# An interleaved attention and MLP kernel: another fixed table of order, engine choices and buffer places

## The chip, the cores and the metric

The kernel runs on one core of a Trainium2 chip. The metric is the device time of one execution in microseconds (us). The time before is the median of 3 runs, 1171.26 us (1171.18 to 1172.04). A core has a matrix engine (TensorE, PE in the profile; its weight loads are PEld), three engines for other arithmetic (VectorE or DVE, ScalarE or ACT, GpSimd or POOL), and a queue that issues transfers (SyncE or SP, SPq in the profile).

## What is computed

Two kinds of layer alternate on x, 2048 rows by 512 features in fp32. `_layernorm` subtracts the mean of a row and divides by its standard deviation.

```python
def _A_ref(x, wqkv, wo):                     # H = 32 heads of Dh = 16
    W, dil = 8, 2
    q, k, v = (x @ wqkv).reshape(B, S, 3, H, Dh).transpose(2, 0, 3, 1, 4)
    idx = pos[:, None] - (arange(W) * dil)[None, :]    # 8 earlier rows, every 2nd
    logits = einsum("bhsd,bhswd->bhsw", q, k[idx]) * Dh ** -0.5
    attn = softmax(where(idx >= 0, logits, -1e9))
    return einsum("bhsw,bhswd->bhsd", attn, v[idx]) @ wo     # heads joined

def _B_ref(x, w1, w2, w3, w4):               # F = 1792
    h = gelu(layernorm(x) @ w1)
    # four quarters of the features, moved by +1, -1, +2, -2 rows
    x1 = x + shifted(h) @ w2
    return x1 + gelu(layernorm(x1) @ w3) @ w4

for layer in range(2):
    x = x + _A_ref(layernorm(x), wqkv, wo)
    x = x + _B_ref(layernorm(x), w1, w2, w3, w4)
```

## The kernel before

**Tiling.** The 2048 rows are cut into 4 blocks of 4 tiles of 128 rows. A step number n counts pairs of layer and block, from 0 to 7; "block 3" or `p4[0]` in this text means the step with that n. An fp32 product is made from fp16 parts: a weight, or a transposed activation, is split in a high and a low half (`w_hl`, `wo_hl`, `wq_hl`; `nT`, `xt`, `oT`), and three products, high by high, high by low, low by high, are added up. A tile by a 512x512 weight is so a group of twelve matmuls of 512 columns.

**Stages.** At the start the weights come in, are scaled by a power of two and are split: for w3 and w4, pair by pair (`big_pair`, line 932), the squares are summed into `ss_p`, a matmul with `ones` adds them over the partitions, DVE reads the sum as `mx`, and a scale `inv_p` follows; `small_weight` (line 910) does the same for wo, w1 and w2. `p1_quarters` (line 793) makes q, k and v of block 0 from fp32 weights at once. `p1_stream` (line 854) does so for each later n: it normalises and transposes x to `xt`, runs the qkv groups `mm<-wq_hl,xt` and writes them to a scratch in DRAM (`kvq_d`). `p2_unit` (line 1004) is the attention of one tile, on DVE mostly: it loads the shifted rows (`kv`), multiplies (`prod<-kv,q`), reduces (`L<-prod`), takes the softmax, multiplies again (`prod<-kv,L`) and adds up. For n of 0 and 1 PE does part of the adding, by `mm<-ident,prod`. The attention of one n is called a set here. `p3` (line 1156) is the product with wo (`mm<-wo_hl,oT`), the layernorm, the product with w1 (`mm<-nT,w_hl`), gelu and the row shifts. `p4` (line 1277) is the product with w2 (`mm<-w_hl,h`), the sum `f<-mm,s_w,f` and the second layernorm. `p5` (line 1342) is the MLP: `mm<-nT,w` makes the hidden features, `acc<-w,g` the output.

**Turning a tile.** Every activation must be transposed before a matmul takes it as weights. `split_turned` and `turn_any` (lines 652 and 670) know three ways. In T_PE, PE transposes the fp32 tile in four pieces (`mm<-ident,f`), ACT copies the high half out, PE subtracts it in the bank (`mm<-nT,minus_id`, called the correction here) and ACT copies out what is left. T_SUB transposes on PE too and subtracts on DVE. T_DMA casts the tile to fp16 (`g<-f`), takes the remainder on POOL or DVE (`g<-f,g`) and has SP issue a transposing transfer (`nT<-g`, `xt<-g`, `oT<-g`).

**What sets the order.** The kernel first describes a graph of 3793 operations, each with one or more ways: the engine that does it, or the kind of PSUM bank it uses (`mm` or `acc`). The function `plan` then runs them by a fixed table. A number k in `ORDER` names operation k // 4 and its way k % 4; each engine gets its instructions in the order of the table and runs them in that order (the class `InOrder`, whose `issue` at line 348 is the line of every instruction in the profile, so groups are told apart by tile names). `SLOTS` holds one hexadecimal digit for each buffer: its place in the pool of its kind. `KEEP` names the operation ahead of which `fill` puts warm-up matmuls, and how many; the first 38 (`WARM`) come ahead of everything.

```python
    for b, c in zip(bufs.values(), "".join(SLOTS.split()), strict=True):
        b.t = slots[b.kind][int(c, 16)]
    for k in ORDER:
        o = ops[k // 4]
        if k // 4 in KEEP:
            todo.append(lambda o=o, n=KEEP[k // 4]: fill(o, n))
        todo.append(o.alts[k % 4][1])
```

A buffer in a place waits until all users of the buffer that was there are done, whichever engines they are on. An engine that waits holds up everything behind it in its own order.

Of the kernel before, what the change touches and what calls it, by code (L numbers as in the profile page):

```python
# [238 lines left out]
4116420101235127621133433326510212035335  # L239
"""  # L240

KEEP = {22: 26}


class Buf:
# [65 lines left out]
def plan(ops, slots, fill=None, picks=()):  # L311
# [11 lines left out]
    for k in ORDER:  # L323
        o = ops[k // 4]
        assert o.before | o.order <= done
        done.add(o)
# [1136 lines left out]
```

## Time and profile before

| | |
|---|---|
| median of 3 runs | 1171.26 us |
| the profiled execution | 1171.19 us |
| its span | 1169.4 us |
| its mean granted PE clock | 0.995 |
| busy PE, DVE, ACT, POOL | 1149.4, 893.0, 597.4, 414.0 us |
| DMA | 206.04 MB, mean 176 GB/s |

A row of a group reads: line, engine, operation, tiles (out<-in) and shape, count, then busy time, mean ns of one, and the idle time before them with what ended it. The mean ns of one matmul is longer than its share of the busy time, because matmuls overlap in the array. A row of a timeline reads: start, length, engine, operation, count, and in brackets the idle time before it and what ended that. In the rows of transfers the last number is the median of us from issue to landing.

### The profile page before, as it was taken

Reading aid. Unit: us, or ns where it says so; the run is one execution under the profiler, and the core shown is the slowest. Engines: PE = TensorE matmul, PEld = TensorE weight load, DVE = VectorE, ACT = ScalarE, POOL = GpSimd, SP = SyncE. Lnnn points to the kernel's source line nnn. Section 1 sums busy time; section 2 is a strip of 40 time slices with the busy share of each in tenths; the row PEclk is TensorE's granted clock in tenths of the full one; section 3 lists DMA queues with packets and bytes.
Section 4 is the critical chain, followed back from the end, with each engine's and each line's share of the span. In section 5 each row is a group of like instructions: output and inputs, shape, how many; then the busy total and the mean of one; then the engine's idle time right before and its main releaser. Section 6 shows DMA issues by size and latency. Waiting matters only on the chain.

```text
span 1169.4 us, 15821 instructions
## 1 busy us (share of the span) xinstructions
PE 1149.4 (98%) x5688; PEld 562.9 (48%) x5688; DVE 893.0 (76%) x1074; ACT 597.4 (51%) x1149; POOL 414.0 (35%) x480
## 2 busy tenths in 40 slices
PE   9999999899999999999999999999999999999998
PEld 7545556455444444444444444444444444444554
DVE  6799988999998995499957989999825999325112
ACT  6665657556664656343553456455544564253232
POOL 3555354424345335332523241731332152223000
PEclk9999999899999999999999999999999999999999
DMA  7678986555586737764568488765378466333312
GB/s 252 214 230 281 271 257 207 187 194 178 161 209 186 168 96 184 226 167 127 162 177 282 136 205 219 189 170 155 102 195 216 129 169 194 103 100 86 98 70 99
DMA packets 231990, 206.04 MB, mean 176 GB/s; under 512 B 104108, under 2 KB 157604, under 8 KB 231912
## 3 DMA queue, kind: packets, MB, share of 16 engines
q1 hardware_dynamic: 231036, 204.07, 61.3%
q8 instruction: 44, 0.72, 0.3%
q10 hardware_dynamic: 876, 0.97, 0.2%
q14 instruction: 34, 0.28, 0.1%
HBM read 141.03 MB, written 39.47 MB: 154 GB/s over the span
## 4 chain that ended last, share of the span: by engine, by line
PE 79%; DVE 8%; DMA 7%; issue 2%; ACT 2%; SPq 1%; POOL 1%; DVEq 0%; ACTq 0%; POOLq 0%
PE mm L348 56%; PE acc L348 23%; DMA kvq_d<-ev 3%; DVE prod L348 3%; DVE L L348 2%; DMA q<-kvq_d 1%; SPq L348 1%; DMA kv<-kvq_d 1%; DVE wq_hl L348 1%; ACT junk L348 1%; DMA w<-w 1%; ACT ev L348 0%; DMA h<-in_B_w_dram 0%; DMA w<-g 0%; DVE mx L348 0%
## 5 line engine op out<-in xcount | busy, mean ns | idle before, releaser
L348 POOL TENSOR_TENSOR g<-f,g 128x512 f16<-128x512 f32 (+1 forms) x123 | 175.0, 1430 | 355.4 <-ACT g L348 158.1
L348 PE MATMUL acc<-w,g 128*128 128x512 f16 x1302 | 298.0, 379 | 0.0
L348 PE MATMUL mm<-nT,w 128*128 128x512 f16 (+1 forms) x1344 | 296.7, 374 | 0.9 <-ACT nT L348 0.7
L348 ACT ACTIVATE mm<-mm,s_w 128x512 f32<-128x512 f32 (+2 forms) x158 | 97.9, 622 | 252.9 <-PE mm L348 252.6
L348 PEld LDWEIGHTS <-w 128*128 128x128 f16 x1512 | 142.0, 98 | 155.3 <-issue 4.5
L348 PEld LDWEIGHTS <-g 128*128 128x128 f16 x1398 | 137.3, 98 | 158.9 <-issue 1.9
L348 PE MATMUL mm<-wq_hl,xt 128*128 128x512 f16 x732 | 164.5, 379 | 1.0 <-DVE ev L348 1.0
L348 PEld LDWEIGHTS <-xt 128*128 128x128 f16 x1008 | 98.5, 98 | 116.9 <-issue 1.5
L348 DVE TENSOR_REDUCE L<-prod 128x128 f32<-128x2048 f32 (+1 forms) x44 | 142.5, 3248 | 0.5
L348 DVE TENSOR_TENSOR prod<-kv,q 128x4096 f32<-128x4096 f32 (+1 forms) x32 | 117.9, 3683 | 6.1 <-DMA kv<-kvq_d 3.6
L348 DVE SCALAR_TENSOR_TENSOR g<-mm,c_g,g 128x512 f16<-128x512 f32 (+1 forms) x53 | 39.3, 743 | 83.1 <-ACT g L348 82.0
L348 DVE TENSOR_TENSOR prod<-prod 128x1024 f32<-128x1024 f32 (+2 forms) x56 | 93.6, 1672 | 0.8
L348 DVE TENSOR_TENSOR prod<-kv,L 128x4096 f32<-128x4096 f32 (+1 forms) x23 | 86.2, 3751 | 1.9 <-PE acc L348 1.6
L348 PE MATMUL mm<-wo_hl,oT 128*128 128x512 f16 x384 | 86.6, 379 | 0.4 <-DVE g L348 0.3
L348 PE MATMUL mm<-nT,w_hl 128*128 128x512 f16 x384 | 86.1, 379 | 0.6 <-DVE g L348 0.6
L348 PE MATMUL mm<-w_hl,h 128*128 128x512 f16 x384 | 85.8, 379 | 0.0
L348 ACT ACTIVATE g<-mm,c_g 128x512 f16<-128x512 f32 (+1 forms) x112 | 74.1, 673 | 2.5
L348 PEld LDWEIGHTS <-oT 128*128 128x128 f16 x426 | 41.4, 98 | 49.1 <-issue 1.2
L348 PE MATMUL acc<-wq_hl,xt 128*128 128x512 f16 x276 | 62.5, 379 | 0.0
L348 PEld LDWEIGHTS <-w_hl 128*128 128x128 f16 x384 | 37.5, 98 | 45.9 <-issue 1.3
L348 PEld LDWEIGHTS <-h 128*128 128x128 f16 x384 | 37.5, 98 | 45.2 <-DVE h L348 0.4
L348 ACT ACT_TABLE_LOAD x40 | 51.3, 1283 | 5.3 <-PE mm L348 3.9
(250 smaller groups left out, 1338.5 us busy)
## 6 DMA issues: line engine op xcount, KB each, us to landing
w<-w SPq DMA_DIRECT2D x224, 256.0 KB, 4.2
kv<-kvq_d SPq DMA_DIRECT2D x62, 768.0 KB, 6.5
kvq_d<-ev SPq DMA_DIRECT2D x84, 256.0 KB, 3.6
w<-in_B_w_dram SPq DMA_DIRECT2D x28, 256.0 KB, 3.8
w<-g SPq DMA_DIRECT2D x28, 256.0 KB, 4.9
q<-kvq_d SPq DMA_DIRECT2D x28, 256.0 KB, 4.1
w<-in_A_x_dram SPq DMA_DIRECT2D x16, 256.0 KB, 4.0
x<-in_A_x_dram SPq DMA_DIRECT2D x16, 256.0 KB, 4.7
```

The lines of the kernel that those rows point to most:

```text
L348: i = f(*a, **k).ins
```

## The change

Three tables change and nothing else. `ORDER` has another sequence, and 550 of the 3793 operations have another way. `SLOTS` has other digits. The warm-up matmuls of `KEEP` move from operation 22 (the transposes of tile 0 of block 0) to operation 33 (those of tile 1).

```diff
 ORDER = [int(k) for k in """
-952 16 40 32 37 24 52 956 20 64 29 45 60 48 69 76 196 72 81 209 152 85 158 202 164 160 204 213 168 108 88 114 116 96
...
 SLOTS = """
...
-KEEP = {22: 26}
+KEEP = {33: 26}
```

Among the other ways: 5 of the tiles that PE transposed are now turned by DMA (3 in `p1_stream`, 2 in `p3`), so there are 20 fewer `mm<-ident,f`, 7 fewer corrections by `minus_id`, and 5 more DMA transposes (`nT<-g` 49 to 51, `xt<-g` 17 to 20). In `p4` some tiles change their way in both directions. Of the 32 adds `x<-x,f` DVE does 19 (8 before) and POOL 13 (24 before).

**VectorE, some 60 us in (place B).** These rows of DVE lead to the read of the power sum `ss_p_225` of the second pair of w3 and w4, which is `mx_264<-mm_70` before and `mx_256<-mm_72` after. L is the logits of the first attention set, junk the dump of a square. Before:

```order
L348 SCALAR_TENSOR_TENSOR junk,ss_p_225<-w_292 128x512
L348 TENSOR_REDUCE L_296<-prod 128x16x8 x2
L348 TENSOR_SCALAR inv_w_237<-inv_w_237 128x1 x2
L348 TENSOR_TENSOR L_296<-L_296,maskb 128x256
L348 TENSOR_SCALAR mx_255<-mm_68 128x1
L348 TENSOR_SCALAR mx_264<-mm_70 128x4
L348 TENSOR_TENSOR prod<-kv_273,x_278 128x2048
```

After:

```order
L348 TENSOR_REDUCE L_296<-prod 128x16x8
L348 TENSOR_SCALAR x_286<-acc_270,s_kv 128x128
L348 TENSOR_SCALAR x_287<-acc_270,s_kv 128x128
L348 TENSOR_TENSOR L_296<-L_296,maskb 128x256
L348 TENSOR_REDUCE mx_255<-L_296 128x32
L348 SCALAR_TENSOR_TENSOR junk,ss_p_225<-w_248 128x512
L348 TENSOR_SCALAR x_286<-mm_70,s_kv 128x128
L348 SCALAR_TENSOR_TENSOR junk,ss_p_225<-w_291 128x512
L348 TENSOR_SCALAR mx_267<-mm_72 128x1
L348 TENSOR_SCALAR inv_w_237<-inv_w_237 128x1 x2
L348 TENSOR_SCALAR mx_256<-mm_72 128x4
```

The two reduces stood between the last square and the read, and now stand ahead of the squares. On PE the power sum is still followed by a group of twelve `mm<-wq_hl,g` and then the four transposes that take the same bank (`mm_70` before, `mm_72` now).

**TensorE, from `p4[0]` to `p5[0]` (place C).** These are the rows of PE from the last w2 matmul of block 0 to its first MLP matmul; the nT of the last row is the second layernorm of three tiles. Before:

```order
L348 MATMUL mm_72<-w_hl,h_254 128x512
L348 MATMUL mm_68<-ident,f_289 128x128 x4
L348 MATMUL mm_66<-ident,f_265 128x128 x4
L348 LDWEIGHTS minus_id
L348 MATMUL mm_68<-nT_287,minus_id 128x512
L348 LDWEIGHTS minus_id
L348 MATMUL mm_66<-nT_287,minus_id 128x512
L348 MATMUL mm_72<-ident,f_265 128x128 x4
L348 LDWEIGHTS minus_id
L348 MATMUL mm_72<-nT_287,minus_id 128x512
L348 LDWEIGHTS w_248
L348 MATMUL mm_72<-nT_287,w_248 128x384
```

After, with the other eleven matmuls of each qkv group left out:

```order
L348 MATMUL mm_72<-w_hl,h_253 128x512
L348 LDWEIGHTS minus_id
L348 MATMUL mm_68<-oT_268,minus_id 128x512
L348 MATMUL mm_70<-ident,f_260 128x128 x4
L348 MATMUL mm_72<-ident,f_264 128x128 x4
L348 LDWEIGHTS minus_id
L348 MATMUL mm_70<-nT_288,minus_id 128x512
...
L348 MATMUL acc_273<-wq_hl,xt_301 128x512
...
L348 MATMUL mm_72<-nT_288,minus_id 128x512
...
L348 MATMUL acc_275<-wq_hl,xt_301 128x512
...
L348 MATMUL mm_72<-nT_288,w_282 128x384
```

Two groups of qkv matmuls of a later block now stand between the corrections and the first MLP matmul, and the third tile's transposes and correction are gone from PE: that tile is turned by DMA. The row with `oT_268` is a correction of another tile that stood elsewhere before.

More of the change, by code (lines that the diff above doesn't have):

```diff
@@ L44 @@
 ORDER = [int(k) for k in """
[174 rows of a table removed]
[174 rows of a table added]
 """.split()]
 SLOTS = """
-714320110422530132632313030201112100021110201233010283600023337540332314113200107520031330113335011321210130511060200
-033425024357010002022155361243020107010413322144030501023153041530040501022033214603060201013641123535000403031451354
-606405061200100320032130101033011002000201021020032110110131100100120000000041202201213205030120111330203002000103111
-202110113311023200103331112000011311002111011011023001100130112120102000112211002030000000000353203302115110220111211
@@ L225 @@
-002410133032051240311003001120101030020114011011101122000053012321112030100620102300100131002100000000213612120002140
-251203111005010131310010502103102120011220011133001111010211001121100601120001100220106301000100221310132624800231510
-316300262010031202230010351030413033473020136050151623604407110453541326207336221235053740211526326130401116351020020
-630533204020021000132300020001012242051022051651040123336361235323425735006011633001705422423532376210011555604242334
-300000124201001103331011010300021304021111020102000103203101530102010133000113211210010120101160010100113313100614267
@@ L230 @@
-305216002231013320404012124301115200311020422530336735031204041120335045471106300210371360650234211022614103630457035
-200000020001021310421110030303010311111001000010010110222100400213001020301010312023011232301111021010102121010423815
-102300204212012220536203122005104000511120232410035401610230150710325204031246043150576165351165103020245041121575231
-300000011000120203611202151331010214021100011002121011303011231103210020200113101001100310201000012111013231101226204
-100102101161000120512200214100200310206530034220430431230126122050517140340605103623117151522630022422476013251540320
@@ L235 @@
-600003100002100102620011041053001301102101030110020102213101110122310130130106211212011113001023000221000313100507381
-202316100130031100100112301203313530136210133430330335120137110422051343670302115310574060212464102151204232540173202
-650623011052002220233005052030110002055302044101223005342045132072303101401222720160310516642523202572132133463653701
-521400374830401330034000000042631021510331213003330023543053013023021112361230070321353012423411603223151622733523211
-4116420101235127621133433326510212035335
+103760101101101233421522032510210011220112322133201131603101254031112251231200200482002031202100121200403352407010204
@@ new lines @@
+000335115643070102031014412234000702010322051606040500022623124545030401011133022016070002011001343551050406021622412
+355631713211001100002110100103321122020201033201102000100101201110030000000051341002200115004301210001502133011020141
+353310211100022111022010120121012110133120010110022211103230102131103300103010023100000000050130011113010132230010130
+303301133000141342203313301122201122221106311131001002200001020031011132001421221211121331112000000000112022111032100
+331310000002031221300011502330111110001000100212001032112330113223101530000310013111006001123101020101131735230531310
@@ new lines @@
+005201143040410302420531300022033022403060317161150443435526134470416032112057511043233030005135467040232354041620500
+230115003152021201321520420630023443022501012570542310634220261130114200576162131322416010112710536342402611621403131
+500003024003011010521013011101120311035302101121321010112011000022301020310101211012011000101063012330102131011313758
+302314101213053020321103020205113210122300014120526724332012135512243043063021233570236064201515041730164261730451201
+000002016102101513411313020351130204001010110101120101212011520202001112001001312122100003201160020110113213100110214
@@ new lines @@
+103006001343030500431311230302200320231530135410332435730215231620253102202434051171246062502160051702251161641321252
+000001131001111312120200110030101105130011100021131013031010001203101001220116112221100321201113010000111300010225763
+202214002001043400502201203000011200412130434510020320132014351760120261530016320700423235070134354512376141143560200
+500004004212010411611013030362011202124213021121200103210010210200010113030110302112010032010062102310112013010308201
+002304303032033310432211035001103020201330135400026701212304101103553010300267265243017040343176032502624304163304220
@@ L240 @@
+367542043132023600414101342011300042161304115102353304216152301210645632732120134231224735560320710123653623750526420
+120225380230000220235003142013121310530311101022443001310020441000033143302310360100421221170310502503371101642213162
+2133000205703134124206216020322116705234
 """
-KEEP = {22: 26}
+KEEP = {33: 26}
 class Buf:
```

347 rows, old and new, of the table ORDER are left out of this document.

## The prediction

> **What bounds the kernel now.** I read the page first (the totals and the chain), then TensorE's waits, then clock and busy time by windows, then the two places that the windows pick out.
>
> ```profile
> span 1169.4 us, 15821 instructions
> PE 1149.4 (98%) x5688; PEld 562.9 (48%) x5688; DVE 893.0 (76%) x1074; ACT 597.4 (51%) x1149; POOL 414.0 (35%) x480
> PE 79%; DVE 8%; DMA 7%; issue 2%; ACT 2%; SPq 1%; POOL 1%; DVEq 0%; ACTq 0%; POOLq 0%
> ```
>
> PE is busy for 98% of the span and holds 79% of the chain. Only two things can shorten this kernel: less matmul work, or less of the 20 us of idle PE (1169.4 − 1149.4) and of the half-clock time that idling brings. The profiled execution took 1171.19 us, so 1.8 us lie around the span; it stands 0.07 below the median of 1171.26, and I make the sum against it.
>
> ```profile
> PE mm L348 <- DVE mx L348: 2.4, 1, 2.4
> PE mm L348 <- POOL f L348: 2.3, 3, 1.1
> PE mm L348 <- ACT nT L348: 1.8, 3, 0.7
> ...
> 60.00:70.00 10.00, 7.62 (x38) 4.02 (x36) 8.67 (x15) 3.47 (x9) 6.31 (x5) 0.83 0.69 204
> ...
> 210.00:220.00 10.00, 6.78 (x34) 3.50 (x31) 9.45 (x10) 7.66 (x19) 6.67 (x11) 0.89 0.82 280
> 220.00:230.00 10.00, 9.31 (x50) 5.67 (x50) 7.94 (x9) 3.88 (x6) 0.56 (x1) 0.76 0.27 65
> ...
> 350.82:409.29 58.47, 58.47 (x275) 26.80 (x273) 54.16 (x45) 30.33 (x52) 26.39 (x20) 1.00 0.67 177
> 935.00:1000.00 65.00, 65.00 (x305) 29.76 (x304) 59.65 (x54) 29.57 (x53) 23.70 (x16) 1.00 0.62 172
> ```
>
> The first three rows are TensorE's longest waits. The others are windows: length, then busy time of PE, weight load, DVE, ACT and POOL, then granted clock. From 60 to 70 us, and from 210 to 230 us, PE idles and the clock is below one; in the other two it never stops. There DVE is busy 54.16 of 58.47 us and 59.65 of 65: a second engine stands just behind PE.
>
> **Place B, 58 to 69 us**: PE, then DVE.
>
> ```profile
> 58.58 2.11 PE L348 MATMUL mm<-wq_hl,g 128*128 128x384 f16 x12
> 63.08 0.63 PE L348 MATMUL mm<-ident,f 128*128 128x128 f32 x4 [2.38 <-DVE mx L348]
> 63.54 3.32 PE L348 MATMUL acc<-wq_hl,g 128*128 128x384 f16 x12
> ...
> 57.12 0.69 DVE L348 SCALAR_TENSOR_TENSOR junk<-w 128x512 bf16<-128x512 f32 x1 [4.76 <-ACT junk L348]
> 57.74 4.47 DVE L348 TENSOR_REDUCE L<-prod 128x128 f32<-128x2048 f32 x2
> 62.71 0.22 DVE L348 TENSOR_SCALAR mx<-mm 128x1 f32<-128x1 f32 x2
> ```
>
> Four transposes need the bank in which a power sum lies until DVE has read it as mx, and DVE first does two reduces of 4.47 us. PE stands for 2.38 us; then twelve matmuls that took 2.11 us take 3.32. The window's clock of 0.83 is a loss of 0.17 × 10 = 1.7 us, so place B costs 2.4 + 1.7 = 4.1 us.
> [...]
>
> **Place C, 213 to 224 us**, the hand-over from the first block's w2 matmuls to its MLP.
>
> ```profile
> 213.77 0.60 PE L348 MATMUL mm<-ident,f 128*128 128x128 f32 x4
> 215.30 0.66 PE L348 MATMUL mm<-ident,f 128*128 128x128 f32 x4 [0.93 <-POOL f L348]
> ...
> 216.64 0.38 PE L348 MATMUL mm<-nT,minus_id 128*128 128x512 f16 x1 [0.47 <-ACT nT L348]
> 218.15 1.12 PE L348 MATMUL mm<-ident,f 128*128 128x128 f32 x4 [1.14 <-POOL f L348]
> 219.95 0.58 PE L348 MATMUL mm<-nT,minus_id 128*128 128x512 f16 x1 [0.69 <-ACT nT L348]
> 221.22 5.60 PE L348 MATMUL mm<-nT,w 128*128 128x384 f16 x23 [0.69 <-ACT nT L348]
> ```
>
> Three tiles are normalised, transposed and corrected one after the other, with nothing between. From 213.77 to 221.22 go by 7.45 us.
>
> **The change part by part.** It alters 550 of 3793 choices of engine or bank, the order and the places. I costed the issue lists of both kernels by counts and the mean durations of this trace.
>
> *PE work.* Five tiles fewer are transposed on PE: 20 fp32 transposes and 7 corrections by minus_id disappear.
>
> ```profile
> L348 PE MATMUL mm<-ident,f 128*128 128x128 f32 x120 | 18.0, 281 | 4.9 <-DVE mx L348 2.4 <-POOL f L348 2.3
> L348 PE MATMUL mm<-nT,minus_id 128*128 128x512 f16 x8 | 3.1, 404 | 1.2 <-ACT nT L348 1.2
> ...
> 984.79 3.24 PE acc L348 x15
> 988.03 2.59 PE mm L348 x12
> ```
>
> A pipelined 512-column matmul costs 2.59/12 = 0.216 us. Four transposes took 0.60 with the last one's 0.281 exposed, so the pitch is (0.60 − 0.28)/3 = 0.107. The least is 20 × 0.107 + 7 × 0.216 = 3.6 us. By the group means (18.0/120 = 0.150 and 3.1/8 = 0.39) it is 3.0 + 2.7 = 5.7, but those means hold the gaps and slow clock that I count apart. I take **−3.6**, 5.7 being the upper end.
>
> *Place B.* After the change DVE does the reduces earlier, and between the second square and the read of its power sum stand only three tiny instructions. The read is through before PE has done the 2.11 us group ahead of its transposes: the 2.4 us of wait and 1.7 of clock go. What is late next is the square: if DVE again starts the first at 57.12, the second ends at 57.12 + 2 × 0.69 + 0.34 (a small scaling between them) = 58.8, and PE, at the power sum by 58.2, waits 0.6. So **−3.5**; bounds 0 (DVE later by the 4.1) and −4.1.
>
> *Place C.* PE now does three w2 groups on end, then a left-over correction, two tiles' transposes, and between their corrections two groups of twelve qkv matmuls. The third tile goes by DMA.
>
> ```profile
> L348 POOL TENSOR_TENSOR g<-f,g 128x512 f16<-128x512 f32 x111 | 163.0, 1476 | 316.0 <-ACT f L348 144.4 <-ACT g L348 134.8 <-DVE g L348 15.6
> L348 ACT ACTIVATE g<-f 128x512 f16<-128x512 f32 x42 | 26.0, 625 | 19.4 <-POOL f L348 8.4 <-DVE mx L348 4.5 <-DVE f L348 3.2
> ...
> nT<-g SPq DMA_TRANSPOSE x49, 3.5
> oT<-g SPq DMA_TRANSPOSE x24, 3.7
> ```
>
> Before, of the 7.45 us, PE's work is 3 × (0.43 + 0.22) = 1.95, so 5.5 are lost. In the window from 220 the clock costs 0.24 × 10 = 2.4 us, 0.6 of which fell before 221.22; 1.8 more makes 7.3. After: the third tile is normalised 218.15 − 213.77 = 4.4 us after the last w2 group; cast 0.6, remainder on POOL 1.5 and DMA transpose 3.5 make 10.0 us. PE meanwhile has 0.22 + 2 × 0.43 + 2 × 0.22 + 2 × 2.59 = 6.7 us of work. It waits 3.3 at full clock: **−4.0**. Bounds: −1.6 where the waits, in two or three pieces, halve the clock again (2.4), and −7.3 where all is covered. I stand near the middle: each piece is shorter than the one at B.
>
> *DVE work and the attention sets.*
>
> ```profile
> 441.51 0.75 DVE L348 SCALAR_TENSOR_TENSOR g<-o,c_o,g 128x512 f16<-128x512 f32 x1
> ...
> 447.69 2.53 PE L348 MATMUL mm<-wo_hl,oT 128*128 128x512 f16 x11
> ...
> 996.45 0.75 DVE L348 SCALAR_TENSOR_TENSOR g<-o,c_o,g 128x512 f16<-128x512 f32 x1
> ...
> 1000.81 2.54 PE L348 MATMUL mm<-wo_hl,oT 128*128 128x512 f16 x11
> ...
> L348 DVE TENSOR_TENSOR x<-x,f x8: 675/684/1354, 339.5 to 1132.8; 128x512 f32<-128x512 f32 x8
> ```
>
> A stage's wo matmuls need the set's last DVE output and its DMA transpose. In block 3 that is 441.51 + 0.75 + 3.7 = 446.0, 1.7 us before PE came to it; in block 7 it is 996.45 + 0.75 + 3.7 = 1000.9, against 1000.81: no slack. Up to block 3's set, DVE loses 4.1 us of work (a weight's square of 2.3 us and several evictions move to ACT). PE wants to be there 11.1 us sooner (3.6 + 3.5 + 4.0). DVE can follow by 4.1 of work, 1.7 of slack and as much of its 4.76 us stall as goes; the shortfall is 11.1 − 10.6 = 0.5 with the stall gone and 5.3 with all of it left. I take **+1.5**, near the first, since other DVE work precedes the squares now.
> From block 3's set to block 7's, DVE gains 10.2 us of work. Eight more x<-x,f adds than before lie there, 8 × 0.69 = 5.5 us, taken from POOL; the rest is final scalings and casts. PE's own work up to block 7 rises by 5.1 over the same stretch, as matmuls move ahead, and that covers half. In blocks 5 and 7 the set has no slack; I take **+2.5** for what remains, between 0 (qkv matmuls start the sets earlier, as in block 7, by 6 us) and 5.1 (10.2 − 5.1).
>
> *The rest.* Eleven adds fewer on POOL and some on ACT cost nothing: POOL is at 35% and ACT at 51%. SP issues five more transposes, covered by its long idle time; what they cost without that cover is C's third tile and rival 3. At the start x(0,1) is loaded first and the warm-up moves with it; PE waits for the same first loads, ±1 us. About ten waits of 0.2 to 0.9 us between 89 and 186 us stay as many, I assume; ±3.
>
> **Sum**: −3.6 − 3.5 − 4.0 + 1.5 + 2.5 = −7.1; 1171.2 − 7.1 = **1164.1 us**.
>
> **Rivals.** *(1) All cover, nothing new waits*: 1171.2 − 11.1 = 1160.1. For it: PE is gapless from 245 us on, so time won early stays won. Against: DVE at 54.16 of 58.47.
> *(2) DVE sets the pace to block 3*: the early win ends at 4.1 + 1.7 = 5.8; with +2.5 later, 1167.9. For it: the same row.
> *(3) Slower: DVE's later sets.* The 10.2 us come through whole as PE waits before wo in blocks 5 and 7, on top of case 2: 1171.2 − 5.8 + 10.2 = 1175.6. It decides from the point where those waits exceed what is won early, some 8 us. For it: no slack in block 7, DVE at 92%. Against: 5.1 us more PE work lies ahead of that point.
> [...] The row of x<-x,f shows up to 1354 ns against a median of 684, once in eight. If each of the eight later adds were held so, they would cost 8 × 0.67 = 5.4 us more and case 3 would be 1181.
> *(4) The waits only move*: PE's stops at B and C go, others of like size open among the new places of buffers, and 3.6 us of less work meet 2.5 of late sets: 1170.1. For it: ten small waits in the first 190 us, where nearly every choice changes.
>
> **How the numbers follow.** A measurement here tells 0.2%, 2.3 us, from nothing. Forecast 0.42 (its own range 1161 to 1167), case 1 0.14, case 2 0.12: faster 0.68. Case 4, same, 0.15. Case 3, slower, 0.17. The range goes from 1157 (case 1 with 3 us of the small waits won) to 1175, just short of case 3.
>
> **What would show it.** Right: no wait for DVE mx and full clock from 60 to 70 us; at 210 to 230 us less than 3.5 us of idle and a clock near one; 100 `mm<-ident,f`; PE at block 3's wo 9 to 11 us sooner. Wrong: a clock below one in a window that had one; waits of `mm<-wo_hl,oT` for the DMA transpose in blocks 3, 5 or 7 above 3 us; DVE idle time in the first 245 us longer than before's.

## The result and the profile after

The changed kernel takes 1152.95 us (median of four runs, 1151.77 to 1153.87); the kernel before, measured beside it, 1171.22. The ratio is 0.9845, with a 95% interval of 0.9827 to 0.9862: 18.3 us less. The direction was forecast; the time was not: 1164.1 was the forecast and 1157 the lower end of its range. The profiled execution took 1153.17 us.

The first rows of the page of the changed kernel: the span, busy time by engine, granted clock in 40 slices, the chain of work.

```profile
span 1151.4 us, 15775 instructions
PE 1138.7 (99%) x5661; PEld 558.4 (49%) x5661; DVE 890.5 (77%) x1077; ACT 600.7 (52%) x1156; POOL 389.2 (34%) x474
PEclk9999999999999999999999999999999999999999
PE 79%; DVE 10%; DMA 4%; issue 3%; POOL 2%; ACT 2%; SPq 0%; DVEq 0%; POOLq 0%; ACTq 0%
```

PE's idle time fell from 20.0 us to 12.7 (1151.4 − 1138.7), and its busy time by 10.7, although only 3.7 us of matmul work went: most of the rest of those 10.7 is matmuls that no longer run at half clock. In the kernel before the granted clock was 0.50 for 3.41 us from 64.28 us on and for 6.83 us from 217.88 on, with PE busy for 8.6 of these 10.2 us; in the changed kernel it was 1.00 from 6.19 us until the last matmul. TensorE's longest waits now:

```profile
PE mm L348 <- DVE f L348: 1.8, 1, 1.8
PE mm L348 <- ACT ev L348: 1.7, 2, 0.9
PE mm L348 <- POOL f L348: 1.3, 1, 1.3
```

None is a wait for DVE's `mx`, and ACT's `nT` is down to 0.2 us. Windows of the kernel before, and after it the same windows of the changed kernel (length, busy time of PE, weight load, DVE, ACT and POOL, then granted clock, DMA share, GB/s):

```profile
40.00:70.00 30.00, 27.61 (x148) 14.90 (x147) 22.57 (x32) 16.74 (x41) 16.94 (x15) 0.94 0.77 243
70.00:200.00 130.00, 127.01 (x697) 70.51 (x696) 118.52 (x157) 86.35 (x179) 64.24 (x73) 1.00 0.84 255
200.00:250.00 50.00, 45.45 (x259) 27.03 (x258) 46.06 (x40) 26.97 (x49) 16.55 (x19) 0.93 0.54 175
```

```profile
40.00:70.00 30.00, 30.00 (x167) 16.29 (x167) 24.63 (x40) 22.30 (x52) 19.23 (x17) 1.00 0.77 254
70.00:200.00 130.00, 127.75 (x708) 71.88 (x705) 121.22 (x157) 89.98 (x190) 60.30 (x79) 1.00 0.89 270
200.00:250.00 50.00, 48.88 (x290) 29.16 (x291) 49.58 (x42) 28.83 (x52) 12.74 (x15) 1.00 0.67 216
```

From 40 to 70 us PE does 19 matmuls more in the same 30 us, from 200 to 250 us 31 more in 50, and the clock is full in both. At place B, first DVE and then PE of the changed kernel:

```profile
49.18 2.28 DVE L348 TENSOR_REDUCE L<-prod 128x128 f32<-128x2048 f32 x1
...
51.64 2.28 DVE L348 TENSOR_REDUCE L<-prod 128x128 f32<-128x2048 f32 x1
...
57.19 0.69 DVE L348 SCALAR_TENSOR_TENSOR junk<-w 128x512 bf16<-128x512 f32 x1 [0.96 <-ACT junk L348]
...
58.89 0.15 DVE L348 TENSOR_SCALAR mx<-mm 128x4 f32<-128x4 f32 x1
```

```profile
58.38 2.11 PE L348 MATMUL mm<-wq_hl,g 128*128 128x384 f16 x12
60.32 0.60 PE L348 MATMUL mm<-ident,f 128*128 128x128 f32 x4
```

The reduces are through by 54 us, the power sum is read at 58.89, and the transposes that need its bank follow the group ahead of them without a gap. At place C, PE of the changed kernel, from the two tiles' transposes to the first MLP matmul:

```profile
200.05 1.09 PE L348 MATMUL mm<-ident,f 128*128 128x128 f32 x8 [1.29 <-POOL f L348]
...
201.61 2.75 PE L348 MATMUL acc<-wq_hl,xt 128*128 128x512 f16 x12
...
204.41 2.75 PE L348 MATMUL acc<-wq_hl,xt 128*128 128x512 f16 x12
207.98 6.01 PE L348 MATMUL mm<-nT,w 128*128 128x384 f16 x36 [0.82 <-ACT ev L348]
```

Three waits of 1.29, 0.25 and 0.82 us are left, 2.4 together, where the prediction had 3.3. The last of them ends with the third tile's transposing transfer, although the row names ACT's `ev`. SyncE issues that transfer here:

```profile
204.77 1.27 SPq L348 DMA_TRANSPOSE nT<-g  x1
```

The trace has its landing at 207.85 us, and in all eight traces of the changed kernel and its variants PE goes on 0.13 to 0.14 us behind this landing, also in a_third_group below, where `ev` had ended 1.1 us before.

For each matmul I compared the moment it starts with the sum of all matmul work ahead of it at full clock; where that lag shrinks, time is won. A stop costs its wait and some 0.2 us more by this tally, since the matmul behind it overlaps none before it (one of 512 columns lasts 379 ns, and on end they start every 216 ns): the kernel before lost 4.8 us from 70 to 190 us, 3.0 of them idle time, in ten stops of 0.08 to 0.64 us. The gain lies here, each share good to some 0.3 us:

| | predicted | measured |
|---|---|---|
| matmul work | −3.6 | −3.7 |
| start, to 37 us | 0 (±1) | +0.1 |
| place B | −3.5 | −4.2 |
| small waits, 70 to 190 us | 0 (±3) | −3.9 |
| place C | −4.0 | −4.4 |
| all later stages | +1.5 + 2.5 | −1.2 |
| after the last matmul | 0 | −0.9 |
| sum | −7.1 | −18.2 (the spans differ by 18.0) |

So 5.2 us of the miss lie in the two terms for DVE, 3.9 in the small waits, 2.0 in the rest.

### The profile page after: what moved, and what is told of

It is laid out like the page before. It is cut to its first block, busy times and chain, and to the rows that moved or that the text cites. A ratio compares the mean times of both kernels' runs of the same rounds, so it can differ in the third digit from the quotient of the medians.

```text
span 1151.4 us, 15775 instructions
## 1 busy us (share of the span) xinstructions
PE 1138.7 (99%) x5661; PEld 558.4 (49%) x5661; DVE 890.5 (77%) x1077; ACT 600.7 (52%) x1156; POOL 389.2 (34%) x474
## 4 chain that ended last, share of the span: by engine, by line
PE 79%; DVE 10%; DMA 4%; issue 3%; POOL 2%; ACT 2%; SPq 0%; DVEq 0%; POOLq 0%; ACTq 0%
PE mm L348 55%; PE acc L348 25%; DVE prod L348 4%; DVE L L348 2%; DMA kvq_d<-ev 1%; POOL g L348 1%; DMA w<-in_A_x_dram 1%; DVE g L348 1%; DMA kv<-kvq_d 1%; DVE mx L348 1%; DMA w<-w 1%; DVE wq_hl L348 0%; DVE x L348 0%; SPq L348 0%; DVE f L348 0%
## 5 line engine op out<-in xcount | busy, mean ns | idle before, releaser
L348 DVE TENSOR_TENSOR prod<-kv,q 128x4096 f32<-128x4096 f32 (+1 forms) x27 | 100.8, 3736 | 10.5 <-DMA q<-kvq_d 5.9
L348 DVE TENSOR_TENSOR prod<-prod 128x1024 f32<-128x1024 f32 (+2 forms) x56 | 91.0, 1626 | 0.9
L348 DVE TENSOR_TENSOR prod<-kv,L 128x4096 f32<-128x4096 f32 (+1 forms) x21 | 77.5, 3690 | 0.4
L348 PE MATMUL acc<-wq_hl,xt 128*128 128x512 f16 x264 | 59.7, 379 | 0.0
L348 DVE SCALAR_TENSOR_TENSOR x<-mm,s_wo,x 128x512 f32<-128x512 f32 x32 | 23.8, 747 | 41.2 <-PE mm L348 37.7
```

The costliest lines, as they stand in the source:

```text
L348: i = f(*a, **k).ins
```

## The experiments

A difference in us to the changed kernel is taken from the ratios, which hold both against the kernel before on the same chip; with their intervals it is good to some 2 us. Names with b_ are the kernel before with a piece of the change, names with a_ the changed kernel with a piece undone or a delay added. A number k in the diffs is an entry of `ORDER`: operation k // 4, way k % 4.

### Place B: the two reduces

**The reduces moved forward in the kernel before** (b_reduces_first): the operations 452 and 454 ahead of the square.

```diff
+1808
+1816
 ...
-1808
-1816
```

> The kernel before, with one move: the two L reduces of place B (4.47 us of VectorE) go ahead of the square junk<-w in front of which VectorE stood for 4.76 us, so they fill that stall. Theory 'lead' (TensorE's stops of the first 250 us all follow from VectorE being late): place B's 4.1 us go, and with VectorE 4 to 5 us ahead the small waits between 70 and 190 us go too, 3 us or more of their 4.9: 1163 to 1165 us. Rival 'local' (each stop has its own cause): place B alone, 4.1 us: 1167, with the small waits as before.

Measured: 1168.91 us, ratio 0.997 (0.9959 to 0.9982). Place B's wait is gone and the clock there is 1.00, but of the 4.1 us not all arrive: 3.5 by the ratio, 2.6 by the spans (1169.4 to 1166.8). The waits between 70 and 190 us, in the kernel before (two of six rows):

```profile
PE mm L348 <- DVE prod L348: 0.7, 2, 0.4
PE mm L348 <- ACT junk L348: 0.6, 1, 0.6
```

with the reduces moved (two of five):

```profile
PE mm L348 <- POOL f L348: 1.2, 1, 1.2
PE mm L348 <- ACT junk L348: 0.9, 1, 0.9
```

and in the changed kernel, the only row:

```profile
PE mm L348 <- ACT ev L348: 0.9, 1, 0.9
```

In sum 2.7, 3.0 and 0.9 us. Time won at B did not remove the small waits. The traced run loses 0.7 us at its start, by the tally, which is most of the 0.9 between the two figures above.

**The reduces put back in the changed kernel** (a_reduces_late): operations 452, 454, 455 and 456 behind the second square, as they were before.

> The changed kernel, with place B put back: the two L reduces and the mask and maximum behind them go after the second square junk<-w and ahead of the read of the power sum, as they stood before. 'Local': the four transposes wait again for DVE mx, 2.5 to 3.5 us, and half clock follows for 3.4 us, 1.7: 1157 to 1158. 'Lead': VectorE is later by the 4.8 us too, and with no slack left before block 1 TensorE waits there as well, 3 us more: 1160 to 1161.

Measured: 1158.52 us, ratio 0.9883 (0.9867 to 0.9898). PE at place B:

```profile
64.30 0.56 PE L348 MATMUL mm<-ss_p,ones 128*128 128x4 f32 x2 [4.89 <-DVE mx L348]
64.72 3.42 PE L348 MATMUL mm<-wq_hl,g 128*128 128x384 f16 x12
```

The place costs 4.89 of wait and 1.3 of slow clock in these twelve matmuls; the change adds 4.5 us to the time by the ratios, 5.8 by the spans. By the tally of the traced run the place costs 6.6 us and the start 1.0, and 1.8 come back later. No small wait came back behind it (0.5 us between 70 and 190). Both runs say the same: the small waits do not hang on a lead won at B.

### Place C: the qkv groups, the third tile, one bank

**The two qkv groups put between the corrections of the kernel before** (b_qkv_between): operations 968 and 965 moved back.

```diff
-3873
 ...
-3860
 ...
+3873
 ...
+3860
```

(Their copies out of PSUM, 3878 and 3864, move with them.)

> The kernel before, with only place C changed: the two groups of twelve qkv matmuls that stood among the w2 groups are done 10 to 18 us later, one between the two corrections and one between the third tile's transposes and its correction; that tile is still turned by TensorE. Of the 7.3 us lost there about 2 of waiting stay, since 5.2 us of work now fill the chain, and the clock stays whole: 5.3 us less, 1166. Rival (the cover only moves the wait, because the two groups' results come 18 us later): the gain of 5.3 is given back before 450 us, 1170 to 1172.

Measured: 1175.3 us, ratio 1.0025 (1.0015 to 1.0035): some 3 us more. The old waits of C shrink, and a new one stands ahead of them. PE, then DVE:

```profile
210.11 2.40 PE L348 MATMUL mm<-w_hl,h 128*128 128x512 f16 x7 [4.57 <-DVE oT L348]
```

```profile
205.97 2.29 DVE L348 TENSOR_REDUCE L<-prod 128x128 f32<-128x2048 f32 x1
...
209.38 0.68 DVE L348 TENSOR_TENSOR oT<-mm,oT 128x512 f16<-128x512 f32 x1
```

The second w2 group has the bank that `oT<-mm,oT` still reads, and that read stands in DVE's queue behind a product and a reduce. In the kernel before the two qkv groups had covered this; taken away from here to cover C, they leave it open.

**Both moves** (b_both).

> The kernel before with both moves, the reduces ahead of the square and the two qkv groups at place C. 'Local': the sum of the two runs alone, 4.1 + 5.3 = 9.4, 1162. 'Lead': 3 to 4 us more than that, 1158 to 1159. If VectorE sets the pace up to block 3's set, as the prediction's case 2 had it, the sum is cut to some 6 us: 1165, with waits of mm<-wo_hl,oT showing.

Measured: 1171.98 us, ratio 0.9998 (0.9986 to 1.0009). The gain at B and the loss at C cancel; the wait for `oT` is there again (4.56 us at 198.89). The trace is of the fastest of its ten runs, 1167.8 us.

**Both moves and one place of a buffer** (b_three): the bank of that w2 group goes from place 1 to place 0, one digit of `SLOTS`.

> b_both with one place of a buffer changed besides: the bank of the w2 group that the moved groups pushed against goes from place 1 to place 0. By 'the new wait of 4.57 us in b_both was the bank's, so order and place belong together': that wait and the half clock behind it are gone and the time is 1162 to 1166. By 'the chain through VectorE is late whatever bank the group has': a wait of 3 to 5 us stays between 198 and 212 us and the time is that of b_both, 1168 to 1172.

Measured: 1168.81 us, ratio 0.9973 (0.9963 to 0.9983), some 3 us less than b_both. PE, then DVE:

```profile
207.36 4.44 PE L348 MATMUL mm<-w_hl,h 128*128 128x512 f16 x12 [2.64 <-DVE f L348]
```

```profile
206.56 0.73 DVE L348 SCALAR_TENSOR_TENSOR f<-mm,s_w,f 128x512 f32<-128x512 f32 x1
```

The time lies where the second theory had it, though the wait is shorter than its 3 to 5 us. One bank's place is worth some 3 us by the medians, and 1.9 at the wait itself; but the next user of a bank, `f<-mm,s_w,f`, stands right behind `oT` in the same DVE queue, so 2.64 of the 4.56 us stay, with a stretch of slow clock behind them (twelve matmuls in 4.44 us, 2.75 in the same trace at full clock). The small waits of 70 to 190 us sum up to 4.3 here: moves at B and C alone do not bring the changed kernel.

**The two groups taken from C in the changed kernel** (a_qkv_away): operation 968 to ahead of the w2 groups, 965 to behind the first MLP matmuls.

> The changed kernel, with place C's cover taken out: one of the two qkv groups goes back among the w2 groups, the other behind the second MLP group; the third tile is still turned by DMA. If the cover is what gained at C, TensorE waits for that tile 5.2 us longer and the clock halves (2 us or more): 1158 to 1160. If the gain at C came from the DMA turn or from engines that were earlier: 1154 at most. The runs on the kernel before showed a wait of w_hl,h for DVE oT that the groups had covered there (4.6 us); one group is back at that place here, so it says nothing of this one unless that wait shows now.

Measured: 1159.85 us, ratio 0.9897 (0.9877 to 0.9917), +6.1 us.

```profile
207.28 0.44 PE L348 MATMUL mm<-nT,minus_id 128*128 128x512 f16 x1 [2.26 <-ACT nT L348]
211.24 5.54 PE L348 MATMUL mm<-nT,w 128*128 128x384 f16 x24 [3.51 <-ACT ev L348]
```

The second tile's correction waits for ACT again, the first MLP matmuls for the third tile's transfer (it lands at 211.10; `ev`, which the row names, is not what they wait for), and the matmuls behind run at half clock (the clock from 200 to 250 us is 0.93). By the tally C costs 6.6 us in this trace, the start 1.0, and 1.8 come back later. The cover at C is worth more than the 4.4 that the place had gained.

**A third group at C** (a_third_group): one more qkv group, operation 1007, behind the last w2 group, to cover the DMA turn of the third tile.

> The changed kernel with one more group of twelve qkv matmuls (2.59 us) moved from some 176 us to the start of place C, ahead of the first transposes, where TensorE waits 1.29 us for POOL f. If the chain of the third tile (10.0 us) sets place C, more work ahead of it covers 1.3 to 2 us of waits: 1151. If the group covered something at its old place, as the groups did on the kernel before: 1153 or slower.

Measured: 1162.1 us, ratio 0.992 (0.9895 to 0.9945), +8.8 us.

```profile
215.92 4.32 PE L348 MATMUL mm<-nT,w 128*128 128x384 f16 x13 [4.80 <-DMA nT<-g]
```

The third tile's transfer now lands at 215.78 us, in the changed kernel at 207.85. The group's own copy out of its bank stands in ACT's queue (202.71 us) ahead of the third tile's square, so POOL begins that tile's remainder at 207.69 instead of 203.58, and the transfer is issued at 209.37 instead of 204.77. And where the group stood, from 148 to 178 us, there are two new waits (0.47 and 1.02). A group is only cover where the chain that it covers does not itself become later.

### The other ways, and the turns by DMA

**498 of the 550 other ways on the old order and places** (b_ways); the other 52 would put two live buffers in one place.

> The kernel before's sequence and places with 498 of the 550 other engine and bank choices of the change (the rest would put two live buffers in one place): 25 tiles turned by TensorE as after the change and 10 corrections, 19 adds on VectorE. Theory 'order' (lead or local): only the 3.8 us of matmul work go (20 transposes at 0.107 and 8 corrections at 0.216), while B and C stay, since the sequence is the old one: 1167, give or take 3. Rival 'ways' (the other engine choices bring the gain): 1156 or less.

Measured: 1298.74 us, ratio 1.1076 (1.106 to 1.1093). Its longest waits (two of many, 114 us in all):

```profile
PE mm L348 <- DMA nT<-g: 24.6, 4, 10.7
PE mm L348 <- ACT junk L348: 11.6, 3, 9.8
```

Neither expectation was near it.

**Five tiles turned by DMA in the kernel before** (b_turns_dma), the third tile of C among them:

```diff
-3961
+3962
-3965
+3964
 ...
-5517
+5519
-5521
+5520
```

(and three more tiles likewise.)

> The kernel before, with five of the tiles that the change takes from TensorE turned by DMA here too (two of p1_stream, one of p3[1], the third tile of p4[0], one of p4[6]) and nothing else moved: 20 transposes and 2 corrections fewer, 20 x 0.107 + 2 x 0.216 = 2.6 us of matmul work. If the matmul work is what counts, 1169. If the DMA way needs the order that covers it: at place C the third tile comes 10.0 us after the last w2 matmul instead of 4.4, with nothing in between, so TensorE waits 4 to 5 us more there and the clock stays at half longer; other tiles wait too: 1174 or more.

Measured: 1192.37 us, ratio 1.0183 (1.0148 to 1.0219). At C:

```profile
229.21 3.04 PE L348 MATMUL mm<-nT,w 128*128 128x384 f16 x9 [6.88 <-DMA nT<-g]
```

The matmul work saved is 2.6 us (3.7 in the change), but nothing covers the 6.88 us until the transfer lands. There are three more long stops: 3.06 us at 148.4, put down to ACT's `ev`, 3.51 at 305.9, to another `nT<-g`, and 7.83 at 975.9, where the profile names no releaser. The last w2 matmul ended at 219.24 us (214.76 + 4.48), so the third tile came 10.0 us behind it: the prediction's figure for this tile was 10.0.

### VectorE: the adds, and delays put into its queue

**The adds of the residual, DVE or POOL.** a_adds_pool gives the 32 adds `x<-x,f` of the changed kernel to the engines that had them before (24 on POOL); b_adds_dve gives those of the kernel before to the engines of the change (19 on DVE).

```diff
-4845
+4844
-5785
+5784
 ...
```

> The changed kernel with the 32 adds x<-x,f on the engines of the kernel before (8 on VectorE, 24 on POOL). The prediction charged late sets with 2.5 us, mostly for these adds on VectorE: if that was real, 1150 to 1151. If VectorE's 8.6 us for them lie where it is idle: 1153, no change. If choices fit only the order they stand in, as the run with the old order and the new choices suggests: POOL's 1.3 us an add, against 0.77, delays what follows in its queue, 1155 or more.

> The kernel before with the 32 adds x<-x,f on the engines that the change gives them (19 on VectorE, 13 on POOL), all else as it was. In the changed kernel the adds on VectorE were worth 4.5 us. If they are worth it by themselves (POOL comes sooner to the remainders g<-f,g that the MLP waits for): 1167 to 1169. If they are worth it only in the order made for them: 1171, or slower by up to the prediction's 2.5 us where VectorE is without slack (blocks 5 and 7), 1174.

Measured: a_adds_pool 1157.49 us, ratio 0.9875 (0.9859 to 0.9891), +3.5 us; b_adds_dve 1174.2 us, ratio 1.0015 (0.9998 to 1.0032), no gain. In a_adds_pool PE waits for POOL; one such row, and the group of the adds on POOL (in the changed kernel it is x13, 1301 ns):

```profile
838.17 2.33 PE L348 MATMUL acc<-w,g 128*128 128x512 f16 x10 [1.50 <-POOL g L348]
```

```profile
L348 POOL TENSOR_TENSOR x<-x,f 128x512 f32<-128x512 f32 x24 | 35.8, 1497 | 21.2 <-DVE f L348 21.2
```

POOL is busy for a third of the span, and yet at these moments it is late: adds in its queue stand ahead of the work that leads to the remainders `g<-f,g` that PE or a DMA turn waits for. In the chain that leads to the row above stand two adds on POOL (1.71 us at 823.11, 1.27 at 828.87); the last remainder came 4.9 us later than in the changed kernel (836.96 against 832.05), while PE's matmuls of this stage were 2.1 us later (829.77 against 827.71). On DVE the adds take 0.77 us each and delay nothing that shows. In the traced run the start plays no part: PE's stop near 10 us is longer here (2.63 against 1.83 us) but ends at the same time (12.58 and 12.53).

**A delay at 45 us** (a_dve_late): two more reduces, whose results nothing uses, in DVE's queue ahead of the first attention set's products. The delays of this and the next two kernels are made so:

```diff
+    def hold():
+        for _ in range(2): V.tensor_reduce(late[:, :16], at(ones, [...]), AX.X, ALU.add)
 ...
+        if k // 4 in LATE: todo.append(hold)
```

> The changed kernel with two reduces of ones more on VectorE, 128x2048 and some 2.28 us each, ahead of the first attention product at 45 us; their result is used nowhere. It measures the slack that VectorE has over the first 250 us. If VectorE sets the pace (the prediction's case 2): 3.5 to 4.6 us longer, 1156.5 to 1157.5, with the wait at mm<-wo_hl,oT of block 1 or 3 or at mm<-ident,prod. If it has slack: 1153 to 1154.

Measured: 1159.53 us, ratio 0.9894 (0.9876 to 0.9912), +5.7 us.

```profile
58.05 4.43 PE L352 MATMUL mm<-wq_hl,xt 128*128 128x512 f16 x10 [4.85 <-ACT x L352]
```

(L352 is the line that issues every instruction in this kernel.) A delay of 4.6 us shows once, at full size, with slow clock behind it (ten matmuls in 4.43 us), and never again: PE's waits between 70 and 190 us are 0.5 us. At 45 us DVE has no slack; 10 us on, PE and DVE keep their distance whatever the moment.

**A delay ahead of set 7** (a_set7_late), before its first product.

> The changed kernel with two unused reduces of 2.28 us each on VectorE ahead of the first product of block 7's attention. The prediction said that this set has no slack. If so, 4.6 us on VectorE make TensorE wait 3.5 to 4.6 us at block 7's mm<-wo_hl,oT: 1157. If the set has slack after the change: 1153 to 1154. An end that comes later by more than 4.6 us would say that the wait also halves the clock.

Measured: 1155.19 us, ratio 0.9858 (0.9833 to 0.9884), +1.5 us, not clear of noise. It tells little: the two reduces fell into a stretch of 3.71 us in which DVE waits for the load of `kv`, so the set began only 2.0 us later, of which some 1.3 came from earlier in the program. PE did not wait at block 7's wo.

**A delay inside set 7** (a_set7_mid), before the last product with `kv`, where DVE has no idle time.

> The kernel after, with two more reduces of 2.28 us (results unused) put into DVE's queue inside set 7, before the last product of the set's first half (about 972 us), where DVE showed no idle time. By 'the sets have no slack' (the prediction's reading of the late sets): the set ends 4.6 us later, TensorE waits about 4.6 us at mm<-wo_hl,oT of block 7 (988 us), perhaps with a stretch of half clock, and the time is 1157 to 1161. By 'DVE's lead in the set covers it': no wait there, 1153 to 1154.

Measured: 1156.0 us, ratio 0.9867 (0.9845 to 0.9889), +2.6 us (2.8 by the spans), of which the start has 0.3: the stop near 10 us ends at 12.82 instead of 12.53. PE from block 7's MLP to its wo:

```profile
982.30 1.90 PE L352 MATMUL acc<-w,g 128*128 128x512 f16 x8 [1.32 <-POOL g L352]
...
992.24 2.12 PE L352 MATMUL mm<-wo_hl,oT 128*128 128x512 f16 x9 [0.89 <-DMA oT<-g]
```

Of the 4.6 us that DVE was late, PE felt 0.89 at wo. The other wait is POOL's remainder, in the changed kernel:

```profile
977.39 2.56 POOL L348 TENSOR_TENSOR g<-f,g 128x512 f16<-128x512 f32 x1 [10.02 <-ACT g L348]
```

and here:

```profile
977.50 4.75 POOL L352 TENSOR_TENSOR g<-f,g 128x512 f16<-128x512 f32 x1 [10.11 <-ACT g L352]
```

It begins at the same moment but now lies beside a product of DVE that runs from 976.82 to 981.24, and it ends 1.0 us after that product. So set 7 had slack: PE came to wo 1.85 us later than in the changed kernel (989.89 against 988.04) and waited 0.89 there, so 4.6 − 1.9 − 0.9 = 1.8 us.

## Why the prediction was right in direction and wrong in size

**PE work** (−3.6): right. The row count fell by 27 matmuls and the work by 3.7 us; the lower of the two values was the right one, since the group means hold the stops.

**Place B** (−3.5): right, −4.2. The reservation that the square would be late and cost 0.6 did not come: DVE began the first square at 55.27 instead of 57.12 us, of its 4.76 us stall 0.96 is left ahead of the second, and PE came to the power sum at 58.24 without a wait. In b_reduces_first, where nothing else had moved, PE waited 0.23 us there.

**Place C** (−4.0): right, −4.4. PE runs dry and waits for the DMA turn of the third tile, as forecast, but for 0.82 us, with 1.54 in two waits ahead of it, instead of 3.3: the transfer landed 9.3 us behind the last w2 matmul (207.85 − 198.54), where the sum had 10.0. No stop halved the clock (1.00 from 200 to 250 us). What the prediction did not see is what this cost elsewhere: the two groups were already cover for another wait (b_qkv_between). In the changed kernel the three w2 groups run on end without that wait; b_three shows a bank's part in this, 1.9 to 3 us, and the rest was not tried.

**"DVE loses 4.1 us of work", "DVE can follow by 4.1 of work, 1.7 of slack and as much of its 4.76 us stall as goes", +1.5**: this step failed. DVE up to block 3's wo, before and after:

```profile
0.00:447.40 447.40, 434.61 (x2257) 234.40 (x2258) 402.68 (x504) 269.74 (x539) 199.42 (x238) 0.99 0.69 206
```

```profile
0.00:430.90 430.90, 423.89 (x2226) 229.70 (x2227) 397.64 (x502) 272.73 (x548) 175.34 (x230) 1.00 0.71 217
```

PE is there 16.5 us sooner, not 11.1 less 1.5. DVE's work fell by 5.0 us, near the 4.1; but its idle time fell by 11.4 (44.7 to 33.3), not by 4.76 at most. I had taken only the one long stall for idle time that could go. The kernel before had 40 us more of it. Rows of its waits of DVE up to there:

```profile
DVE junk L348 <- ACT junk L348: 7.0, 2, 4.8
DVE x L348 <- PE mm L348: 4.2, 4, 1.7
DVE g L348 <- ACT g L348: 2.1, 2, 2.0
```

In the changed kernel the first is 1.0 us and the other two are below 0.7; others came or grew (3.9 us for POOL's `inv_p`, 3.3 for a load), and the balance is the 11.4. Summed by what DVE waited for, PE went from 8.6 to 2.5 us, ACT from 18.7 to 7.7, POOL from 4.3 to 8.3 and transfers from 7.7 to 9.3. DVE waits for ACT and PE as these wait for DVE, so its idle time is no fixed part of the way to block 3, and a share of 54 in 58 us does not say that DVE sets the pace. The delay at 45 us shows both sides: DVE is on the path at that point, and behind it the two move together without a further wait there.

**"From block 3's set to block 7's, DVE gains 10.2 us of work", "In blocks 5 and 7 the set has no slack", +2.5**: failed twice. The stretch from block 3's wo to block 7's, before and after:

```profile
447.40:1000.60 553.20, 550.94 (x2551) 249.28 (x2549) 444.08 (x470) 267.38 (x489) 189.81 (x205) 1.00 0.66 178
```

```profile
430.90:987.80 556.90, 555.48 (x2573) 251.42 (x2572) 448.46 (x479) 270.25 (x491) 189.44 (x205) 1.00 0.66 179
```

DVE's busy time rose by 4.4 us, not 10.2, and PE's by 4.5, so it was covered. I had costed counts by old mean durations; DVE's instructions of the same form were shorter in the changed kernel, by 4.9 us in sum over the span (56 `prod<-prod` went from 1672 to 1626 ns each, and with the adds back on POOL it is still 1629). The traces show what the means hold: the 128x1024 ones that began with POOL idle took 1217 ns before (18 of them) and 1222 after (22), those that began while POOL was inside an instruction 1674 (10) and 1947 (6). Of all 56, 17 began so before and 13 after. A mean duration thus holds the meetings with POOL of its own schedule; why these became fewer stays open. And "no slack" was read from one subtraction with a median transfer time; the delay inside the set measured 1.8 us, in the changed kernel.

**"Eleven adds fewer on POOL cost nothing"**: true as far as it goes, but I had put the adds down as DVE's loss alone. They are a gain of some 3.5 us in the changed kernel, for the reason that a_adds_pool shows, and none in the kernel before. The busy share of POOL, 35%, said nothing on this.
For long adds the prediction weighed 5.4 us against the change, eight times the 0.67 us between the longest of the old adds on DVE and their median. The traces show how seldom an add was so long: two of the 19 on DVE took 1.50 and 1.52 us (one of the 8 before, 1.35), all three began while POOL was inside an instruction and ended 0.55 us behind its end, and the others took at most 0.72. That is some 1.7 us, not 5.4. In a_set7_mid it was POOL's `g<-f,g` that took longer, 4.75 us instead of 2.56, beside a product of DVE.

**"About ten waits of 0.2 to 0.9 us … stay as many"**: failed, −3.9. They were of 0.08 to 0.64 us, and only one of 0.9 us and one of 0.13 are left between 70 and 190 us. The runs exclude that time won at B removed them (b_reduces_first, a_reduces_late), and a delay of DVE at 45 us did not bring them back (a_dve_late). What is left is that order, ways and places are others at each of these spots; which choice removed which wait, I did not try, so this cause is argued and not shown.

**The rivals.** Case 1, all cover and nothing new waits, 1160.1 with a chance of 0.14, was the nearest; with the small waits added it would have been 1156. Its ground, "PE is gapless from 245 us on", was not quite so: the kernel before has five waits of 0.12 to 1.00 us between 481 and 806 us. Cases 2 and 3, DVE sets the pace, fell with the two steps above. Case 4, waits only move, is what b_qkv_between, b_both and b_adds_dve did on the old table; the whole table did not. Of the marks named beforehand, the clock, the waits for `mx` and the 100 transposes came out as for the forecast; PE at block 3's wo 16.5 us sooner lay outside its 9 to 11.

**What stays open**: the pieces done alone on the old table bring −3.5 (the reduces), +2.9 (the qkv groups), +1.8 (the adds, not clear of noise) and +21 us (the DMA turns), nothing like their parts in the whole. Undone alone in the changed kernel, the first three cost 4.5, 6.1 and 3.5 us, which with 3.7 of matmul work is 17.8 of the 18.3; but each of them also undoes covers that other pieces count on, and in the traces of the first two some 1.0 us each arose at the start, so that this sum may be near by chance. Which choices removed the small waits, and why DVE's instructions met POOL's less often, is not settled.

## What to carry to other kernels

When two engines run nearly full side by side, do not charge one's added work to the other's path before asking what its idle pieces wait for: pieces that wait for the first engine shrink with it (here DVE's waits for PE, up to block 3's wo, from 8.6 to 2.5 us). Before a matmul group is moved to cover a wait, look what it covers now, down to who reads the bank that the next group needs and what stands ahead of that reader in its queue. A piece of such a table, tried alone, told here neither the size nor the sign of its part in the whole.

## What was unexpected in the hardware

**A stop need not be long to halve the clock, and a long one need not do it.** The 2.64 us at 204.7 us in b_three is followed by a half-clock stretch of 3.413 us; so is a stop of 1.94 us at 10.6 us in a_reduces_late (granted clock 0.86 from 8 to 20 us), while stops of 2.63 us (a_adds_pool) and 2.88 us (a_set7_mid) at the same place left it at 1.00. The half-clock stretches that end within a span last 3.413 us or a multiple of it (in the kernel before 3.413 us from 64.28 us on and 6.827 from 217.88; 6.827 us behind the stop of 4.85 us in a_dve_late, so up to 3.4 us on top), and within a trace they begin on a grid of 3.413 us. Cut up along this grid, the sixteen traces have 5421 windows. All 46 in which PE was idle for 2.0 us or more were followed by a window at half clock, 7 of the 27 with 1.5 to 2.0 us were, and none of the 5348 with less; in the kernel before and the changed one alone, 675 windows, it was all 4, one of 2 and none of 669. So the half clock went here with how much of one window was idle: the 2.64 us lay in one window, the 1.94 too, while the 2.63 and the 2.88 us were split over two, 1.54 and 1.09, 1.53 and 1.35.

**A longer stop need not cost more.** The stop of PE at some 10 us was 1.83, 1.94, 2.63 and 2.88 us long (changed kernel, a_reduces_late, a_adds_pool, a_set7_mid) in kernels whose tables are the same up to there, but it ended at 12.53, 12.53, 12.58 and 12.82 us. What differs is when the clock became full: the warm-up matmuls follow each other every 213 ns until 6.19, 5.96, 4.66 and 4.65 us, and every 109 ns from then on. With the clock full earlier, PE is sooner at the same wait and stands there longer. What the start can cost is the half clock behind the stop, by the tally some 1.0 us in a_reduces_late and in a_qkv_away.
